# Two x blocks on ScalarE's DMA queue, and the last block's gate quarters in one piece

## The chip, the cores and the metric

The kernel runs on one core of a Trainium2 chip. The metric is the device time of one execution in microseconds (us); the median of three runs before the change is 233.98 us (233.82 to 234.45).

The core has five engines that run side by side, each through its own list of instructions in order: TensorE (PE in the profile, with PEld for its weight loads), VectorE (DVE), ScalarE (ACT), GpSimd (POOL) and SyncE (SP), which here only issues DMAs. ScalarE can issue DMAs as well; its queue is ACTq in the profile, SyncE's is SPq. Both queues are worked off by the same 16 DMA engines.

## The reference

Two branches are computed from x (2048 rows, 640 columns) and added to it. xn is the layer norm of x over its columns.

```python
xn = _layernorm(x, axis=-1)
return x + _A_ref(xn, A_k, A_v, A_shift_k, A_ssm_k, A_ssm_D) + _B_ref(xn, B_w_gate, B_w_up, B_w_down)
...
g = jnp.einsum("bsd,df->bsf", x, w_gate)
u = jnp.einsum("bsd,df->bsf", x, w_up)
h = _sigmoid(g) * u
return jnp.einsum("bsf,fd->bsd", h, w_down)
```

Branch B (the einsums, in which x stands for xn) is a gated layer of width 1728. Branch A shifts k by 0 to 3 rows with four taps a column, multiplies by v, convolves the result along the rows with a kernel as long as the sequence (in the reference by FFT), adds a term with D, and multiplies by xn.

## The kernel before

The 2048 rows are held as 16 blocks of 128 rows, and the blocks in four groups of four. For each group the kernel makes xn, turns it so that columns lie on the partitions (xnT, which has room for one group and four blocks in it), multiplies by the gate and up weights in 14 column groups of 128 (`product`, L267: five matmuls over 640 columns = five chunks of 128), takes the sigmoid of the gate product on ScalarE (`gate_ev`, L278), multiplies it by the up product on VectorE (`up_ev`, L285), and multiplies the result by the down weights (`down_mm`, L309). Branch A runs between these: a long convolution made of matmuls by tables, with transposes through DRAM, in five chunks of 128 columns.

From L543 on the order of all work is written out by hand: `chains` holds lists of steps, and a long string of letters (ORDER) takes the next step of one list after another. The change touches nothing of it. What it touches lies ahead of that, in the start (L501 to L540):

- x's blocks 0 and 1 are loaded in two halves each, one half from SyncE and one from ScalarE (L501 to L503). Block 2 is loaded whole by SyncE and block 3 whole by ScalarE (L504, L505). Behind them SyncE issues the first weights: gate and up for columns 0 to 255, then gate and up for 256 to 511 (L506 to L508; the DMAs are at L177 and L180 in `load_w`). All later loads are SyncE's too.
- `busy(10)` (L522) runs ten matmuls on zeros while the first data is on its way.
- L523 to L529: for blocks 0 to 3, VectorE takes the statistics of the block (`ln_stats`, L200, two instructions), normalises the block before it (`ln_xn`, L217), and combines the statistics (`ln_aggr`, L204); GpSimd makes the reciprocal root (`ln_pow`, L212).
- `turn(i)` (L517) transposes block i on PE in five matmuls against the identity (`xn_mm`, L242, tile pt) and copies them to xnT on ScalarE in two pieces, chunks 0 to 2 and chunks 3 and 4 (`xn_ev`, L246).
- L532 to L537: `quarters(u, i, lo, hi)` (L255, matmuls at L262) computes a quarter of four products, namely block i's 128 rows for the first two column groups (fc 0 and 1), with gate weights for u = 0 and up weights for u = 1, over chunks lo to hi - 1. For each block the gate products of chunks 0 to 2 come first, then the transposes of the next block, then the gate products of chunks 3 and 4, then the up products. Each fc has its PSUM tile, pg for gate and pu for up.
- Then `gate_ev` and `up_ev` for the two column groups (L538 to L540), and the ordered part begins with the gate product of the third column group.

The products' PSUM tiles come from a pool with four buffers (`psG`, L92). After the start, all four are taken: two pg and two pu. The third column group's gate product (L271) takes the first one that comes free, which is pg of fc 0, when its sigmoid has read it.

For the second to fourth group, xnT is not made on PE but by DMA transposes that SyncE issues (`xn_turn`, L250), each behind its block's xn.

Of the kernel before, what the change touches and what calls it, by code (L numbers as in the profile page):

```python
# [21 lines left out]
NC = DM // P  # L22
# [35 lines left out]
def kernel(  # L58
# [14 lines left out]
    nc = tc.nc  # L73
    xr = A_q.flatten_outer_dims().rearrange("(p b) d -> p b d", b=NB)
# [30 lines left out]
    x = res.tile([P, NB, DM], BF16, name="x")  # L105
# [19 lines left out]
    sync = nc.sync  # L125
# [113 lines left out]
    def xn_mm(i):  # L239
        xts[i] = pt = psC.tile([P, NC, P], BF16, name="pt", tag="c")  # L240
        for c in range(NC):
            nc.tensor.transpose(pt[:, c, :], xn[:, i, c * P:(c + 1) * P], ident[:])  # L242

    def xn_ev(i):
        for lo, hi in ((0, 3), (3, NC)):
            nc.scalar.copy(out=xnT[:, i, lo:hi, :], in_=xts[i][:, lo:hi, :])  # L246
# [8 lines left out]
    def quarters(u, i, lo, hi):  # L255

        for fc in range(2):
            if i == 0 and lo == 0:
                pgs[u, fc] = psG.tile([P, 512], F32, name=("pg", "pu")[u], tag="g")
            o = u * UP + fc * P  # L260
            for c in range(lo, hi):
                nc.tensor.matmul(pgs[u, fc][:, i * P:(i + 1) * P], lhsT=w[:, c, o:o + P], rhs=xnT[:, i, c, :],  # L262
                                 start=(c == 0), stop=(c == NC - 1))
# [237 lines left out]
    for b in range(2):  # L501
        for i in range(2):
            (sync, nc.scalar)[i].dma_start(x[:, b, 320 * i:320 * i + 320], xr[:, b, 320 * i:320 * i + 320])  # L503
    for i in range(2):  # L504
        (sync, nc.scalar)[i].dma_start(x[:, 2 + i, :], xr[:, 2 + i, :])  # L505
    for lo in (0, 256):  # L506
        for u in range(2):
            load_w(sync, lo, lo + 256, u)  # L508
# [8 lines left out]
    def turn(i):  # L517
        xn_mm(i)
        xn_ev(i)
# [10 lines left out]
    turn(0)  # L530
    busy(2)
    for i in range(4):  # L532
        quarters(0, i, 0, 3)
        if i < 3:
            turn(i + 1)
        quarters(0, i, 3, NC)
        quarters(1, i, 0, NC)  # L537
    for fc in range(2):  # L538
        gate_ev(0, fc)
# [162 lines left out]
```

## Time and profile before

| what | value |
|---|---|
| median of three runs | 233.98 us |
| the profiled execution's own time | 234.07 us |
| its span, first to last instruction | 232.3 us |
| PE busy | 227.5 us (98% of the span), 2200 matmuls |
| DVE busy | 203.4 us (88%) |
| ACT busy | 123.2 us (53%) |
| granted TensorE clock | 1.00 |
| DMA | 56.79 MB, mean 244 GB/s |
| first x half issued, first bytes | 0.72 us, from 1.75 us |
| first gate weights issued, landed after | 2.12 us, 4.7 us |
| first up weights issued, first up product | 2.60 us, 8.02 us |
| first 512-wide product | 12.67 us |

How to read the profile: times are counted from the start of the span. "L262" is line 262 of the kernel as printed above. A tile name such as pg<-xnT,w tells what an instruction writes and reads. The chain of waits is followed back from the last instruction to whatever released it, so that it shows the one path that set the end. A timeline lists instructions in order of time, with start, duration, engine, line and tiles; like instructions are merged (x5), and in square brackets is the idle time before, with what ended it. A matmul's end is modelled, and matmuls overlap in the pipeline: a 128-wide one is shown as 0.22 us, while in a run of them the next begins 0.056 us after the last. So a short wait of PE can lie hidden under the shown end of the matmul before. DMA share is the busy share of the 16 DMA engines; it can be over 1, since packets overlap.

### The profile page before, as it was taken

The page shows a single profiled execution, that of the slowest core. Times are in us where ns is not written, and L with a number is a line of the kernel's source. Part 1 is how long each engine was busy: PE and PEld are TensorE (multiplying, and loading weights), DVE is VectorE, ACT ScalarE, POOL GpSimd, SP SyncE. Part 2 cuts the span into 40 slices and gives each one's busy share as a digit, 9 for nine tenths or more (in the row PEclk, how much of TensorE's full clock was granted, in tenths as well). Part 3 has the DMA queues.
Part 4 walks back from the last instruction along what each step waited for, and adds up shares of the span by engine and source line. Part 5 has one row for each costly group of instructions (what it writes and reads, how often), then busy time and mean ns, then how long its engine had stood idle before and what let it go on. Part 6 is the DMA issues. An engine that isn't in the chain of part 4 may idle for free.

```text
span 232.3 us, 5434 instructions
## 1 busy us (share of the span) xinstructions
PE 227.5 (98%) x2200; PEld 130.7 (56%) x2200; DVE 203.4 (88%) x357; ACT 123.2 (53%) x158; POOL 12.4 (5%) x26
## 2 busy tenths in 40 slices
PE   7899999999999999999999999999999999999995
PEld 2754445877454556667554544478653544446772
DVE  4534799999989999999999999997799999997773
ACT  2533232595355887766775847673556667752000
POOL 5210010040001100000011000000000000000000
PEclk9999999999999999999999999999999999999999
DMA  6999999899999999999999999689999999364784
GB/s 177 321 328 234 265 305 298 210 226 175 337 192 296 265 324 224 265 210 233 302 293 266 262 259 286 193 204 178 302 257 264 274 270 257 114 167 118 228 261 136
DMA packets 96303, 56.79 MB, mean 244 GB/s; under 512 B 55894, under 2 KB 90518, under 8 KB 96022
## 3 DMA queue, kind: packets, MB, share of 16 engines
q1 hardware_dynamic: 95846, 56.12, 93.9%
q8 instruction: 17, 0.28, 0.5%
q10 hardware_dynamic: 432, 0.33, 0.5%
q14 instruction: 8, 0.07, 0.1%
HBM read 36.12 MB, written 18.35 MB: 234 GB/s over the span
## 4 chain that ended last, share of the span: by engine, by line
PE 95%; DMA 2%; SPq 1%; issue 0%; DVE 0%
PE pd L315 27%; PE pg L271 24%; PE pu L271 24%; PE psb L488 4%; PE ps L376 4%; PE ps L374 4%; PE ps L418 3%; PE psa L447 2%; DMA w<-in_B_w_up_dram 2%; PE pg L292 2%; PE pu L262 1%; PE pg L262 1%; SPq L503 0%; PE pt L242 0%; SPq L177 0%; SPq L505 0%
## 5 line engine op out<-in xcount | busy, mean ns | idle before, releaser
L271 PEld LDWEIGHTS <-w 128*128 128x128 bf16 x500 | 46.6, 98 | 54.3 <-issue 4.6
L315 PE MATMUL pd<-wd,hT 128*128 128x320 bf16 (+2 forms) x448 | 66.0, 299 | 0.0
L271 PE MATMUL pg<-xnT,w 128*128 128x512 bf16 x250 | 62.2, 379 | 0.1
L271 PE MATMUL pu<-xnT,w 128*128 128x512 bf16 x250 | 62.2, 379 | 0.0
L315 PEld LDWEIGHTS <-hT 128*128 128x128 bf16 x448 | 41.7, 98 | 18.2 <-issue 2.4
L280 ACT ACTIVATE sig<-pg 128x512 bf16<-128x512 f32 x52 | 31.1, 601 | 30.8 <-PE pg L271 25.5
L286 DVE TENSOR_TENSOR hT<-sig,pu 128x512 bf16<-128x512 bf16 x52 | 34.9, 680 | 11.8 <-PE pu L271 7.3
L232 ACT CAST xz<-ps 128x1024 bf16<-128x1024 f32 x36 | 35.1, 1015 | 15.5 <-PE ps L418 15.4
L232 ACT CAST t<-ps 128x1024 bf16<-128x1024 f32 x24 | 23.7, 1013 | 16.3 <-PE ps L376 14.1
L433 DVE TENSOR_TENSOR xz<-xz 128x2048 bf16<-128x2048 bf16 x20 | 24.4, 1219 | 0.2
L376 PE MATMUL ps<-kvh,S1t 128*128 128x128 bf16 x160 | 21.5, 220 | 0.0
L374 PE MATMUL ps<-kvh,S1t 128*128 128x128 bf16 x160 | 21.4, 218 | 0.0
L354 DVE TENSOR_TENSOR acc<-acc,tmp 128x1024 bf16<-128x1024 bf16 x30 | 20.5, 683 | 0.3
L352 DVE TENSOR_TENSOR tmp<-kx,sc 128x1024 bf16<-128x1024 bf16 x30 | 20.4, 680 | 0.3
L320 DVE TENSOR_TENSOR x<-pd,x 128x320 bf16<-128x320 f32 (+2 forms) x32 | 15.2, 482 | 3.8 <-PE pd L315 3.6
L374 PEld LDWEIGHTS <-S1t 128*128 128x128 bf16 x160 | 15.5, 97 | 2.5
L376 PEld LDWEIGHTS <-S1t 128*128 128x128 bf16 x160 | 15.4, 96 | 2.5
L232 ACT CAST TBt<-ps 128x1024 bf16<-128x1024 f32 x14 | 13.8, 1012 | 4.0 <-PE ps L376 4.0
L200 DVE BATCH_NORM_STATS2 st<-x 128x6 f32<-128x320 bf16 x32 | 13.8, 474 | 2.2 <-DMA x<-in_A_q_dram 2.1
L493 DVE TENSOR_TENSOR yx<-psb,xn 128x512 bf16<-128x512 f32 x20 | 13.7, 687 | 1.4 <-PE psb L488 0.8
L431 DVE STREAM_SHUFFLE xz<-xz 128x512 f32<-128x512 f32 x20 | 14.5, 726 | 0.0
L232 ACT CAST ao<-psa 128x1024 bf16<-128x1024 f32 x9 | 9.0, 1013 | 8.6 <-PE psa L447 6.9
(56 smaller groups left out, 159.0 us busy)
## 6 DMA issues: line engine op xcount, KB each, us to landing
t<-d SPq DMA_DIRECT2D x15, 512.0 KB, 6.4
d<-t SPq DMA_DIRECT2D x13, 512.0 KB, 5.0
d<-TBt SPq DMA_DIRECT2D x7, 512.0 KB, 5.2
d<-ao SPq DMA_DIRECT2D x6, 512.0 KB, 6.5
bi<-d SPq DMA_DIRECT2D x6, 512.0 KB, 5.5
kx<-in_A_k_dram SPq DMA_DIRECT2D x10, 256.0 KB, 6.0
hn<-in_A_ssm_k_dram SPq DMA_DIRECT2D x20, 128.0 KB, 5.3
kvh<-in_A_v_dram SPq DMA_DIRECT2D x10, 256.0 KB, 5.6
```

The lines of the kernel that those rows point to most:

```text
L232: nc.scalar.copy(out=out, in_=in_)
L271: nc.tensor.matmul(pg[:, :], lhsT=w[:, c, u * UP + fc * P:u * UP + (fc + 1) * P], rhs=xnT[:, :, c, :], start=(c == 0), stop=(c == NC - 1))
L280: nc.scalar.activation(sig[fc][:, :], pgs[0, fc][:, :], ACT.Sigmoid)
L286: nc.vector.tensor_tensor(hT[:, fc, :], sig[fc][:, :], pgs[1, fc][:, :], ALU.mult)
L315: nc.tensor.matmul(pd[:, :], lhsT=hT[:, fc, bb * P:(bb + 1) * P], rhs=wd[:, fc, es], start=(fc == 0), stop=(fc == NFC - 1))
L320: nc.vector.tensor_tensor(x[:, 4 * t + bb, es], pds[bb, half][:, :], x[:, 4 * t + bb, es], ALU.add)
L352: nc.vector.tensor_tensor(d["tmp"][:, :, :], kx[:, lo + 3 - m:hi + 3 - m, :], sb(m), ALU.mult)
L354: nc.vector.tensor_tensor(d["acc"][:, :, :], d["acc"][:, :, :], d["tmp"][:, :, :], ALU.add)
L374: nc.tensor.matmul(ps[:, i, 0:P], lhsT=S1[:, b, h, :], rhs=cin[c]["kvh"][:, 0, b, :], start=True, stop=True)
L376: nc.tensor.matmul(ps[:, i, P:2 * P], lhsT=S1[:, b, h, :], rhs=hp[:, b // 2, b % 2, :], start=True, stop=True)
L431: nc.vector.stream_shuffle(z[:, 2, :, :].bitcast(F32), z[:, 1, :, :].bitcast(F32), swap)
L433: nc.vector.tensor_tensor(z[:, 1:3, :, :], z[:, 0:1, :, :].to_broadcast((P, 2, 8, P)), z[:, 1:3, :, :], ALU.mult)
```

## The change

x's third and fourth blocks (2 and 3) are both loaded by ScalarE, behind the two halves that it loads already; SyncE goes from its halves of blocks 0 and 1 straight to the first gate weights. And for the last of the four blocks, which has no next block to transpose, the gate quarters are taken over all five chunks at once: all five chunks of fc 0, then all five of fc 1, where before chunks 0 to 2 of both came ahead of chunks 3 and 4 of both.

```diff
     for b in range(2):
         for i in range(2):
             (sync, nc.scalar)[i].dma_start(x[:, b, 320 * i:320 * i + 320], xr[:, b, 320 * i:320 * i + 320])
-    for i in range(2):
-        (sync, nc.scalar)[i].dma_start(x[:, 2 + i, :], xr[:, 2 + i, :])
+    for b in range(2, 4):
+        nc.scalar.dma_start(x[:, b, :], xr[:, b, :])
...
     for i in range(4):
-        quarters(0, i, 0, 3)
         if i < 3:
+            quarters(0, i, 0, 3)
             turn(i + 1)
-        quarters(0, i, 3, NC)
+            quarters(0, i, 3, NC)
+        else:
+            quarters(0, i, 0, NC)
         quarters(1, i, 0, NC)
```

The number of DMAs, their sizes and the number of matmuls stay as they are.

## The prediction

> **What bounds the kernel now.** I read the page's busy shares and slices first, then the chain of waits over the whole span and over its first 14 us, then DMA in stretches of 0.25 us, then the timelines of the engines at the places that the chain named. The page (PE's slices, and the chain's shares):
>
> ```profile
> PE   7899999999999999999999999999999999999995
> ...
> PE 95%; DMA 2%; SPq 1%; issue 0%; DVE 0%
> ```
>
> TensorE (PE) is nearly always busy, and 95% of the chain that ended last is its own work. What can be won lies where the chain is not PE, and that is its first 8 us. The chain of waits for 0 to 14 us (start, duration, what):
>
> ```profile
> 1.66 0.42 SPq L505
> 2.08 0.04 issue
> 2.12 0.43 SPq L177
> 2.56 0.04 issue
> 2.60 5.37 DMA w<-in_B_w_up_dram
> 7.97 0.05 issue
> 8.02 0.73 PE pu L262 x10
> ...
> 12.10 0.56 PE pu L262 x10
> 12.66 0.01 issue
> 12.67 1.24 PE pg L271 x5
> ```
>
> Read upwards: the first up products start at 8.02, when the first up weights have landed; these were issued at 2.60, behind the gate weights (2.12), behind x's third block (L505, 1.66) on SP's queue. From 8.02 on the chain is PE. The waits list gives PE one wait on a weight DMA before that, 0.5 us at the first gate products (6.89).
>
> **Part 1, x's blocks and SP's queue.** SP issues one DMA less before the weights: 2.12 - 1.66 = 0.46 us. Gate weights go out at 1.66, up weights at 2.14, and so do all later SP issues until the queue is full. If landing follows issue, up lands at 7.51: a gain of 0.46. If the DMA engines are full throughout, no byte arrives sooner in sum, and the gain is 0. The DMA stretches decide (stretch, its length, busy us of PE, PEld, DVE, ACT, POOL, granted clock, DMA share, GB/s):
>
> ```profile
> 3.00:3.25 0.25, 0.25 (x2) 0.01 (x1) 0.15 (x1) 0.00 (x0) 0.03 (x1) 1.00 1.10 192
> 3.25:3.50 0.25, 0.25 (x2) 0.15 (x1) 0.25 (x1) 0.00 (x0) 0.00 (x0) 1.00 0.74 97
> 3.50:3.75 0.25, 0.25 (x2) 0.04 (x1) 0.25 (x2) 0.00 (x0) 0.00 (x0) 1.00 0.78 179
> 3.75:4.00 0.25, 0.25 (x2) 0.11 (x1) 0.24 (x1) 0.00 (x0) 0.00 (x0) 1.00 0.73 261
> ...
> 5.00:5.25 0.25, 0.25 (x2) 0.00 (x0) 0.25 (x1) 0.00 (x0) 0.00 (x0) 1.00 1.07 333
> ```
>
> Between 3.25 and 3.75 the engines move 97 and 179 GB/s, against 333 later: (333 - 97 + 333 - 179) x 0.25 = 98 KB are missing, which is 0.29 us at 333 GB/s. In this dip x's third block is alone at the head of SP's queue, with the gate weights behind it; after the change the gate weights are at the head there. First bytes follow an issue by 1.03 us (first issue 0.72, first bytes from 1.75), so that gate data can flow from about 2.7. I take the **0.29 us** of the dip, between the ends of 0 and 0.46, because it is the room that the rows show.
>
> The Trainium skill ("DMA: Bandwidth & Descriptors", section "Issuing engines are not separate DMA queues") speaks against this part: transfers issued from different engines share the same 16 DMA engines, and a second issuer saves its sequencer's time alone. By it the dip is not filled by a change of queue and the term would be 0 instead of 0.29; the rows from 5.00 on (share over 1) agree with it, the dip does not settle it.
>
> What the step brings with it:
> - ScalarE's queue issues x's fourth block at 2.11 instead of 1.65, and ends at 2.57. ScalarE's next real work is the copy at 5.99, before which it sat idle 3.35 us: cost 0.
> - The fourth block landed at 1.65 + 4.3 = 5.95; its statistics start at 7.03, so it may come 1.08 later. It goes out 0.46 later and now shares the engines with gate weights. If it came as late as the gate weights do today (2.12 + 4.7 = 6.82) it would still be in time: cost 0. Later than 7.03 it holds up VectorE, and, since xn's third block is ready at 8.23 and PE's transposes of it would then start at 8.87 - 0.29 = 8.58, holds up PE from about 7.4 on, one for one.
> - The third block (landed 1.66 + 4.1 = 5.76) ended a VectorE wait of 0.17 at 5.75. It can come a little sooner or later; PE has 0.2 to 0.4 us over at each transpose. Cost 0, with 0.17 either way.
> - What is late next, once the weights come 0.29 sooner: the gate products would start at 6.60, behind the copies of block 0 (the first is done by 6.5). The transposes of block 1 wait for xn (6.55 + 0.43 = 6.98), so they start near 7.05; four more gate products end near 7.55; the up products take their place at 7.73. So the 0.29 goes through; weights ahead by more than about 0.45 would find PE waiting for xn instead.
> - Second weights (256 to 511) land at 3.75 + 6.4 = 10.15, and are needed at 12.67: no effect.
>
> **Part 2, the last block's gate quarters whole.** The 40 gate matmuls stay, 0.056 us apart; the order changes for block 3. Before, chunks 0 to 2 of both column groups come first, then 3 and 4, so that group 0 ends with the eighth matmul; now it ends with the fifth, 3 x 0.056 = 0.17 sooner. That matters, because group 0's sigmoid holds the PSUM buffer of the next product (four buffers, all taken). ScalarE's timeline (start, duration, what):
>
> ```profile
> 11.17 0.38 ACT L246 COPY xnT<-pt 128x256 bf16<-128x256 bf16 x1
> ...
> 12.03 0.60 ACT L280 ACTIVATE sig<-pg 128x512 bf16<-128x512 f32 x1 [0.48 <-PE pg L262]
> ```
>
> The sigmoid ends at 12.63 and the product starts at 12.67, where PE could have gone on at 11.94 + 10 x 0.056 = 12.50: a stall of 0.17 that the list of waits hides, since the last matmul's modelled end lies over it. What is added: chunk 3 of group 0 is reached at 11.38 + 3 x 0.056 = 11.55, and its copy ends at 11.17 + 0.38 = 11.55, so it waits about 0.04 (the step from sigmoid to product). Behind it in PE's queue stand all later products, so they pay it. Net **0.13 us** gained. Bounds: 0.17 if the copy is in time; a loss of 0.1 if it comes 0.2 to 0.3 late (no row shows that).
>
> **What comes after.** A gain at the start counts only if nothing later holds PE. By the spacing of its matmuls PE has one further wait. The timeline of PE (start, duration, what):
>
> ```profile
> 56.28 1.11 PE L315 MATMUL pd<-wd,hT 128*128 128x320 bf16 x7
> 57.44 1.24 PE L271 MATMUL pg<-xnT,w 128*128 128x512 bf16 x5
> ```
>
> Seven matmuls 0.136 apart from 56.28 let the next start at 57.23; it starts at 57.44, 0.21 late. It needs the second row group's xnT, whose last DMA transpose SP issues at 54.7, with 2.8 us to landing for the quickest: about 57.4. So this landing must move too. SP's four transposes start at 49.49, behind xn of VectorE (48.98 + 0.44 = 49.42). VectorE has no gap from 30.21 to there, and its instruction at 30.21 waited for PE's up product (end 30.10). So the landing hangs on PE and moves with it, 0 lost; bounds are the whole gain lost, and 0.21 more gained where it moves by more.
>
> **Sum.** 234.07 (the profiled execution; its span is 232.3, with 1.8 around it) - 0.29 - 0.13 = 233.65. The median of the three runs is 233.98, so that this execution lies 0.09 above it; I give **233.6**. A difference under 0.3% (0.70 us) is about what a measurement of this kernel cannot tell from no change.
>
> **Rivals.**
> - Bytes bind, the queue doesn't (the change doesn't do what it says): SP issues sooner, the weights land when they did. For it: DMA share over 1 from 5.00 to 8.00, and all of x, the gate and the up weights stand before PE's 8.02 in either order. Against: the dip. 234.07 - 0.13 = 233.94. This is also the time by the skill's sentence above.
> - The gain is swallowed at 57.44: xnT's last block lands when it did, for DMA reasons. For: SP's first transpose took 2.47 us to issue where the others took 1.22, so the queue is full there. Against: VectorE's gapless run. 234.07.
> - Slower, by the same place: one more of the four transposes takes the 2.47 us of the first, and the last lands 1.25 later, at 58.65. It decides as soon as the last landing comes after PE's own 57.23 less the gain; then every 0.1 costs 0.1. 234.07 + 1.25 = 235.3.
> - More: up lands by the full 0.46 sooner, the copy is in time (0.17), and xnT beats PE (0.21): 234.07 - 0.84 = 233.2.
>
> **Chances.** Forecast 0.40 (gains of 0.2 to 0.7), bytes bind 0.15, swallowed 0.14, more 0.16, slower 0.15. The first three lie within 0.3%, except 0.02 of the forecast that is faster and 0.01 of the swallowed case that is slower: faster 0.18, same 0.66, slower 0.16. The range goes from the case "more", less 0.2 for what the third x block could add, to 0.6 above the swallowed case, half-way into the slower one: 232.9 to 234.6.
>
> **What the changed profile would show.** Step 1: L177's first issue at 1.66, the wait at the first up products ending near 7.7, no dip at 3.25 to 3.75; x's fourth block's statistics still at about 7.0. Step 2: the first sigmoid 0.13 ahead of its place relative to the last quarter, and no gap at the first 512-wide product. Afterwards: the product at 57.44 near 57.0. Wrong it would be if up's landing stays near 7.97, if VectorE waits for the fourth block, or if the product at 57.44 does not move with the start.

## The result, and the profile after

The changed kernel takes 235.25 us (median of 6 runs, 235.01 to 235.87); the kernel before takes 233.96 us (233.82 to 234.45, 6 runs). The ratio is 1.0058, with a 95% interval of 1.0042 to 1.0074: slower by about 1.3 us. The forecast was 233.6 us, and the range ended at 234.6. The profiled execution of the changed kernel took 235.72 us, with a span of 233.9 us (before 234.07 and 232.3).

The page of the changed kernel, PE's slices and the chain's shares:

```profile
PE   7699999999999999999999999999999999999995
...
PE 94%; DMA 4%; DVE 1%; issue 0%
```

PE is as full as before from the third slice on. What is new stands in the first slices: the chain has 4% of DMA in it, where before it had 2%. The chain of waits of the changed kernel for 0 to 14 us (start, duration, what):

```profile
0.72 2.64 DMA x<-in_A_q_dram
3.35 0.02 issue
3.38 5.94 DMA x<-in_A_q_dram
9.32 0.02 issue
9.34 0.89 DVE st L200 x2
10.23 0.36 DVE xn L217
10.59 0.05 issue
10.63 0.45 PE pt L242 x5
...
11.31 0.56 PE pu L262 x10
```

The up weights are gone from the chain. In their place stand two loads of x, one behind the other: the first half block, issued at 0.72, lands at 3.36; only then, at 3.38, is another load of x issued, and it takes 5.94 us, to 9.32. The timeline of the changed kernel names the second one (start, duration, engine, line, tiles, idle time before):

```profile
1.65 0.46 ACTq L505 DMA_DIRECT2D x<-in_A_q_dram  x1
2.69 0.65 SPq L177 DMA_DIRECT2D w<-in_B_w_gate_dram  x1
3.38 0.40 ACTq L505 DMA_DIRECT2D x<-in_A_q_dram  x1
6.96 0.51 PE L262 MATMUL pg<-xnT,w 128*128 128x128 bf16 x6 [0.53 <-DMA w<-in_B_w_gate_dram]
9.34 0.89 DVE L200 BATCH_NORM_STATS2 st<-x 128x6 f32<-128x320 bf16 x2 [1.74 <-DMA x<-in_A_q_dram]
10.14 0.43 DVE L217 TENSOR_SCALAR xn<-x,mv,rstd 128x640 bf16<-128x640 bf16 x1
10.63 0.45 PE L242 MATMUL pt<-ident,xn 128*128 128x128 bf16 x5 [1.48 <-DVE xn L217]
```

ScalarE issues x's third block (block 2) at 1.65 and ends at 2.11; the fourth (block 3) does not follow there but at 3.38. In between, at 2.69, the second gate weights have gone out on SyncE's queue. (L177 and L180 in `load_w` are the same lines for the first and the second weights; the issue at 1.66, not shown, is the first gate weights'.) VectorE stands 1.74 us at the statistics of block 3. Behind them in its queue is the xn of block 2 (10.14), whose data had long been there, and PE waits 1.48 us for that xn. The first 512-wide product starts at 14.28 instead of 12.67, 1.61 late, and this is still there at the second row group. The timeline of PE in the changed kernel:

```profile
57.89 1.11 PE L315 MATMUL pd<-wd,hT 128*128 128x320 bf16 x7
59.09 1.24 PE L271 MATMUL pg<-xnT,w 128*128 128x512 bf16 x5
```

59.09 less 57.44 is 1.65, and the span is 1.6 longer. So the whole loss is made in the first 11 us, and it is still there at the end.

**Why 3.38.** The compiled order of instructions (place on the engine, line, what it waits for) says it. Before, on SyncE:

```text
3 L177 DMACopy w_82<-in_B_w_gate_dram 128x5x256
4 L180 DMACopy w_82<-in_B_w_up_dram 128x5x256
5 L177 DMACopy w_82<-in_B_w_gate_dram 128x5x256 [waits DMAHW0_49]
6 L180 DMACopy w_82<-in_B_w_up_dram 128x5x256 [waits DMAHW1_49]
```

After, on SyncE and on ScalarE:

```text
4 L177 DMACopy w_82<-in_B_w_gate_dram 128x5x256
5 L180 DMACopy w_82<-in_B_w_up_dram 128x5x256 [waits DMAHW1_49]
...
4 L503 DMACopy x_79<-in_A_q_dram 128x320
5 L505 DMACopy x_79<-in_A_q_dram 128x640
6 L505 DMACopy x_79<-in_A_q_dram 128x640 [waits DMAHW0_49]
```

The compiled program signals the landing of these DMAs by eight semaphores, DMAHW0 to DMAHW7, handed out in turn to the DMAs of both queues. The ninth DMA gets DMAHW0 again and waits until its first user has landed. Before, the ninth was the second gate weights (issued at 3.34, needed at 12.67: no harm). After, it is x's block 3, since in the order in which the semaphores are handed out it now stands behind the second gate weights. So the change moved a wait that was there already to another load, and by it let the second gate weights go out ahead of that load.

### The profile page after: what moved, and what is told of

It is laid out like the page before. It is cut to its first block, busy times and chain, and to the rows that moved or that the text cites. A ratio compares the mean times of both kernels' runs of the same rounds, so it can differ in the third digit from the quotient of the medians.

```text
span 233.9 us, 5434 instructions
## 1 busy us (share of the span) xinstructions
PE 227.7 (97%) x2200; PEld 130.7 (56%) x2200; DVE 203.2 (87%) x357; ACT 123.2 (53%) x158; POOL 12.4 (5%) x26
## 4 chain that ended last, share of the span: by engine, by line
PE 94%; DMA 4%; DVE 1%; issue 0%
PE pd L315 26%; PE pu L271 23%; PE pg L271 23%; PE psb L488 4%; PE ps L376 4%; PE ps L374 4%; DMA x<-in_A_q_dram 4%; PE ps L418 3%; PE psa L447 2%; PE pg L292 2%; PE pu L262 1%; PE pg L262 1%; DVE st L200 0%; PE pt L242 0%; DVE xn L217 0%; DVE x L320 0%
```

## The experiments

The texts on record name the theories by letters. At first: the wait for the semaphore makes block 3 late (W); it is late by the company that it keeps, behind block 2 on one queue and beside the weights on the same DMA engines, whenever it is issued (S); the quarters of part 2 cost the time (Q). Later came: a transfer is served in order of issue, by the bytes ahead of it (F), or by the pieces ahead of it (N); and the landings near 43 us are a floor under any earlier start (D). Ratios are to the kernel before, measured beside it on the same chip, with 95% intervals.

**e1: part 1 alone.** The quarters stay as before.

```diff
-    for i in range(2):
-        (sync, nc.scalar)[i].dma_start(x[:, 2 + i, :], xr[:, 2 + i, :])
+    for b in range(2, 4):
+        nc.scalar.dma_start(x[:, b, :], xr[:, b, :])
```

> Part 1 alone (x's blocks 2 and 3 on ScalarE's queue; gate quarters as before). The trace of the changed kernel shows x's block 3 issued at 3.38 us, not 2.11, and its statistics at 9.34, not 7.03. Theory W (wait): that issue waits for the landing of ScalarE's first x half, since it takes over that DMA's completion semaphore. Rival S (sharing): block 3 would come late on that queue at any issue time, because it shares the DMA engines with the weights. Rival Q (quarters): the slowdown is due to the new order of the last gate quarters. W and S: about 0.12 us slower than the changed kernel, 235.4 us. Q: no slower than before, 234.0 us or less.

Measured: 235.04 us against 234.23, ratio 1.0039 (1.0026 to 1.0052). Block 3 was issued at 3.19 and landed at 8.67; PE waited 1.37 us for xn. The loss belongs to part 1, and the quarters are cleared of it: the intervals of e1 and of the whole change overlap.

**e2: part 2 alone.**

```diff
     for i in range(4):
-        quarters(0, i, 0, 3)
         if i < 3:
+            quarters(0, i, 0, 3)
             turn(i + 1)
-        quarters(0, i, 3, NC)
+            quarters(0, i, 3, NC)
+        else:
+            quarters(0, i, 0, NC)
```

> Part 2 alone (the last block's gate quarters whole; x's blocks as before). W and S: about 0.12 us faster than before, 233.85 us (the first 512-wide product 1.18 us after the last gate quarter's start instead of 1.29). Q: slower by about 1.3 us, 235.2 us.

Measured: 234.12 us against 234.23, ratio 0.9994 (0.9976 to 1.0013). In its profile the first 512-wide product starts at 12.26, 0.41 ahead of the kernel before: 0.11 by the shorter way from the last gate quarter to the product (1.18 against 1.29), 0.30 because the quarter itself began sooner in this execution. Yet the second group's product starts at 57.54, not ahead of 57.44. The timelines of VectorE and PE in this run show where the 0.41 went:

```profile
42.20 1.11 DVE L334 STREAM_TRANSPOSE kvh<-hn 128x512 f32<-128x512 f32 x1 [0.30 <-DMA hn<-in_A_ssm_k_dram]
43.77 0.89 DVE L200 BATCH_NORM_STATS2 st<-x 128x6 f32<-128x320 bf16 x2 [0.45 <-DMA x<-in_A_q_dram]
...
54.72 0.23 PE L374 MATMUL ps<-kvh,S1t 128*128 128x128 bf16 x1 [0.55 <-DVE kvh L357]
```

VectorE waits twice for loads, the second time for x's second group (L133, issued at 35.73 here, at 36.17 before: sooner by 0.44; landed 8.01 later, while before VectorE took it up 7.21 after its issue without a wait). PE then waits 0.55 for VectorE. The expected gain of about 0.12 us in the total is less than the interval can show.

**e3: block 3 with a semaphore of its own.** Changed kernel; ScalarE's warm-up sigmoid (L123) stands behind its DMAs instead of between them, which changes the order in which the semaphores are handed out.

```diff
-    nc.scalar.activation(warm[:, :], mhalf[:, :], ACT.Sigmoid)
...
     for b in range(2, 4):
         nc.scalar.dma_start(x[:, b, :], xr[:, b, :])
+    nc.scalar.activation(warm[:, :], mhalf[:, :], ACT.Sigmoid)
```

> The changed kernel, with the warm-up sigmoid of ScalarE moved behind its four x DMAs. By the compiled order of instructions x's block 3 then has a completion semaphore that no earlier DMA used, and the wait goes to the third weight DMA, as before the change; queues, sizes and order of the x DMAs stay. W: block 3 is issued near 2.1 us, lands by 7.1, the PE stall at its transposes' predecessors is gone; 233.8 us (before less 0.12 of part 2, nothing from the weights, which landed no sooner in the changed kernel). S: block 3 still lands after 8.5 us, 234.8 us or more.

Measured: 234.06 us, ratio 0.9998 (0.9981 to 1.0015). The timeline:

```profile
1.65 1.01 ACTq L504 DMA_DIRECT2D x<-in_A_q_dram  x2
3.16 0.37 SPq L176 DMA_DIRECT2D w<-in_B_w_gate_dram  x1
7.33 0.89 DVE L199 BATCH_NORM_STATS2 st<-x 128x6 f32<-128x320 bf16 x2 [0.43 <-DMA x<-in_A_q_dram]
```

Blocks 2 and 3 go out one behind the other from 1.65 on, the second gate weights wait again (3.16), and VectorE waits 0.43 instead of 1.74. The loss is gone: S, with the same bytes in the same queues, falls. What is left is no gain either. The first product started at 12.46, and then VectorE waited 0.61 for x's second group at 43.76 and PE 0.34 for kvh at 54.71, as in e2.

**e4: the wait put into the kernel before.** A 192-byte load on ScalarE's queue ahead of block 3 makes block 3 the ninth DMA; queues and quarters are those of before. The bytes go to a place that the kernel fills later anyway.

```diff
-    for i in range(2):
-        (sync, nc.scalar)[i].dma_start(x[:, 2 + i, :], xr[:, 2 + i, :])
+    sync.dma_start(x[:, 2, :], xr[:, 2, :])
+    nc.scalar.dma_start(TBt[0:1, 0, 0:3, 0:32], SMd.ap()[0:1, :, :])
+    nc.scalar.dma_start(x[:, 3, :], xr[:, 3, :])
```

> The kernel before, with one DMA of 192 bytes more on ScalarE's queue ahead of x's block 3 (into a place that is loaded over later). Queues as before: block 2 on SyncE, block 3 on ScalarE, weights behind block 2. By the compiled order of instructions, block 3 now is the DMA that has to wait for ScalarE's first x half. W: issued near 3.4 us, lands at 8.5 to 9.3, PE stalls 0.8 to 1.6; 234.7 to 235.5 us. S: as before, 234.0 us.

Measured: 234.07 us, ratio 0.9999 (0.9983 to 1.0015). The expectation failed. The timeline:

```profile
3.15 0.34 ACTq L506 DMA_DIRECT2D x<-in_A_q_dram  x1
3.29 0.52 SPq L177 DMA_DIRECT2D w<-in_B_w_gate_dram  x1
7.75 0.89 DVE L200 BATCH_NORM_STATS2 st<-x 128x6 f32<-128x320 bf16 x2 [1.06 <-DMA x<-in_A_q_dram]
```

Block 3 does wait, and goes out at 3.15, but it lands 4.6 us later (e1: 5.5, changed kernel: 5.9). So the wait is not the whole cause. Two things differ from the changed kernel: block 2 is on SyncE's queue here, and the second gate weights go out behind block 3 (3.29) and not ahead of it (2.69). e5 leaves block 2 on ScalarE's queue and so tells them apart.

**e5: changed kernel, second weights behind block 3.** The same small load, now on SyncE's queue between the first and the second weights, so that the second gate weights wait too.

```diff
     for lo in (0, 256):
         for u in range(2):
             load_w(sync, lo, lo + 256, u)
+        if lo == 0:
+            sync.dma_start(TBt[0:1, 0, 0:3, 0:32], SMd.ap()[0:1, :, :])
```

> The changed kernel with a DMA of 192 bytes more on SyncE's queue, between the first and the second weights. It takes the last unused completion semaphore, so that the second gate weights, too, wait for a landing and go out at about the same time as x's block 3, not 0.7 us ahead of it. The wait of block 3 itself stays (issue near 3.2 to 3.4 us). Putting the wait into the kernel before cost nothing, so the wait alone is not enough. Theory F (first come, first served): both queues' transfers are served nearly in the order of issue, and block 3 lands behind all bytes issued before it; up's landing (1280 KB at 7.97) and block 3's in the kernel before (640 KB at 5.95) give 324 GB/s. F here: 1280 KB up to and with block 3, landing 7.6 to 8.3, PE held 0 to 0.4; 234.0 to 234.3 us. Rival W (the wait alone, on this queue): lands 8.7 to 9.3 as in the changed kernel; 235.2 us.

Measured: 234.08 us against 234.14, ratio 0.9992 (0.9973 to 1.0011). The timeline:

```profile
2.95 0.33 ACTq L505 DMA_DIRECT2D x<-in_A_q_dram  x1
3.57 0.38 SPq L177 DMA_DIRECT2D w<-in_B_w_gate_dram  x1
7.84 0.89 DVE L200 BATCH_NORM_STATS2 st<-x 128x6 f32<-128x320 bf16 x2 [0.96 <-DMA x<-in_A_q_dram]
```

The wait is there (2.95 instead of 2.11), the second weights are behind, and the loss is gone. Block 3 landed at 7.82, as F expected (7.6 to 8.3) and W did not (8.7 to 9.3). It lands 1.50 sooner than in the changed kernel, of which 0.43 is its earlier issue. e3 takes away the wait and with it the overtaking (the second weights going out ahead of block 3); e5 takes away the overtaking and keeps the wait. Either removes the loss. The overtaking without the wait was not tried, so whether it alone would make the loss stays open.

**e6: more bytes ahead.** Changed kernel with the second weights 512 columns wide (640 KB instead of 320 KB each), so that twice as much goes out between the up weights and block 3.

```diff
-    for lo in (0, 256):
+    for lo, hi in ((0, 256), (256, 768)):
         for u in range(2):
-            load_w(sync, lo, lo + 256, u)
+            load_w(sync, lo, hi, u)
...
-    for k in ((load_w, sync, 512, 1024, 0),
-              (load_w, sync, 512, 1024, 1),
+    for k in ((load_w, sync, 768, 1024, 0),
+              (load_w, sync, 768, 1024, 1),
```

> The changed kernel with second weights twice as wide (columns 256 to 767, then 768 to 1023 behind them): 640 KB instead of 320 KB go out between the up weights and x's block 3. Issue of block 3 as in the changed kernel. F: 328 KB more at 324 GB/s, 1.0 us later than in the changed kernel: lands near 9.7 to 10.3; 236.2 us. W: as the changed kernel, 235.2 us.

Measured: 235.31 us, ratio 1.0042 (1.0027 to 1.0057). The timeline:

```profile
9.02 0.89 DVE L200 BATCH_NORM_STATS2 st<-x 128x6 f32<-128x320 bf16 x2 [2.25 <-DMA x<-in_A_q_dram]
```

Issued at 3.18, landed at 8.99: 5.8 us, no more than with half the bytes ahead (5.5 in e1, 5.9 in the changed kernel). F, which asked for 1.0 us more in the landing and in the total, fails: the ratio lies between those of e1 (1.0039) and of the changed kernel (1.0058).

**e7: part 2, and x's second group in two loads.** This asks whether the landings near 43 us swallow the gain of e2. Against e2 the edit is:

```diff
-              (load_x, sync, 1),
+              (load_x, sync, 1, 2),
```

> Part 2 alone, and x's second group of four blocks loaded as two DMAs of two blocks instead of one of four. In the run of part 2 alone, the first 512-wide product came at 12.25 instead of 12.67 us, but VectorE then waited 0.30 for hn and 0.45 for x's second group (statistics at 43.77; 43.38 in the kernel before), and PE 0.55 near 54.7 for VectorE: the gain of the start was gone. Theory D: these landings, set by the bytes of the DMA queue up to there, are a floor that the start does not move. With the first two blocks landing about 1 us sooner the second wait goes, 0.30 is left of hn: 0.1 to 0.4 us faster than part 2 alone, 233.6 to 233.9 us. Rival: the floor is elsewhere (kv of branch A), and this changes nothing, 234.0 us.

Measured: 233.68 us, ratio 0.9981 (0.9965 to 0.9997), the only version whose interval lies wholly below 1. The timelines of VectorE and PE:

```profile
43.01 0.85 DVE L200 BATCH_NORM_STATS2 st<-x 128x6 f32<-128x320 bf16 x2
...
56.03 1.11 PE L315 MATMUL pd<-wd,hT 128*128 128x320 bf16 x7
56.98 1.24 PE L271 MATMUL pg<-xnT,w 128*128 128x512 bf16 x5
```

The statistics start at 43.01 without a wait, and the product starts 0.95 after the seven down matmuls (7 x 0.136), where before it took 1.16. In this execution it is 0.46 ahead of 57.44, and the span is 231.8 against 232.3. Two parts make up the 0.46. The first product came at 12.42, 0.25 ahead of before, and the seven down matmuls too are 0.25 ahead (56.03 against 56.28): this lead was kept. The other 0.21 is the shorter step behind the down matmuls, which e8 shows without part 2 as well.

**e8: the two loads alone**, on the kernel before: the diff of e7, without part 2.

> The kernel before, with x's second group loaded as two DMAs of two blocks. VectorE had no wait at 43.38 in the kernel before. D: no change, 233.8 to 234.0 us. If x's landing already held the kernel before there, up to 0.2 faster.

Measured: 233.84 us, ratio 0.9986 (0.9972 to 1.0000). By the medians the split alone brings 0.30 of e7's 0.46 us, but the intervals of e7 and e8 overlap. Its profiled execution started late (first product at 13.03), so the trace shows one thing only: the product follows the down matmuls by 0.95 here too (56.64 to 57.59), so that this 0.21 belongs to the two loads and not to part 2.

**e9: as many bytes ahead, in longer pieces.** Changed kernel with 320 KB of x, in 128 pieces of 2560 bytes (blocks 4 and 5), issued between the up weights and the second gate weights, which have pieces of 512 bytes.

```diff
     for lo in (0, 256):
         for u in range(2):
             load_w(sync, lo, lo + 256, u)
+        if lo == 0:
+            sync.dma_start(x[:, 4:6, :], xr[:, 4:6, :])
...
-              (load_x, sync, 1),
+              (sync.dma_start, x[:, 6:8, :], xr[:, 6:8, :]),
```

> The changed kernel with half of x's second group (blocks 4 and 5: 320 KB as 128 pieces of 2560 bytes, which is loaded later otherwise) put between the first and the second weights on SyncE's queue. It goes out ahead of x's block 3, where the changed kernel has the second gate weights (320 KB as 640 pieces of 512 bytes); those now go out with block 3. Doubling their bytes at the same number of pieces moved block 3's landing to 8.99, not to the 9.7 to 10.3 of theory F, so F's bytes are not what counts ahead of block 3. Theory N: the place in line is given by pieces (rows to be written), first come, first served. N: block 3 lands at 7.8 to 8.3, little later than with nothing there (7.82); 234.0 to 234.4 us. F: 8.7 to 9.3, as with 320 KB of weights; 235.1 us.

Measured: 235.06 us against 234.75, ratio 1.0031 (1.0013 to 1.0048). The timeline:

```profile
9.20 0.89 DVE L200 BATCH_NORM_STATS2 st<-x 128x6 f32<-128x320 bf16 x2 [2.12 <-DMA x<-in_A_q_dram]
```

Issued at 3.29, landed at 9.18: 5.9 us. Fewer pieces don't help, and N falls.

**e10: half the bytes ahead in as many pieces.** Changed kernel with the second weights in two steps of 128 columns (160 KB each, 640 pieces of 256 bytes).

```diff
-    for lo in (0, 256):
+    for lo, hi in ((0, 256), (256, 384), (384, 512)):
         for u in range(2):
-            load_w(sync, lo, lo + 256, u)
+            load_w(sync, lo, hi, u)
```

> The changed kernel with the second weights cut into columns 256 to 383 and 384 to 511: ahead of x's block 3 go 160 KB of gate weights as 640 pieces of 256 bytes, instead of 320 KB as 640 pieces of 512. N: block 3 lands as in the changed kernel and in part 1 alone, 8.6 to 9.3; 235.0 us. F: half-way to the kernel with nothing there (7.82), 8.2 to 8.5; 234.6 us.

Measured: 235.51 us against 234.75, ratio 1.0035 (1.0016 to 1.0054). The timeline:

```profile
8.76 0.89 DVE L200 BATCH_NORM_STATS2 st<-x 128x6 f32<-128x320 bf16 x2 [1.73 <-DMA x<-in_A_q_dram]
```

Issued at 3.10, landed at 8.74: 5.6 us. That lies in N's range (8.6 to 9.3) and not in F's (8.2 to 8.5), but e9 had already spoken against N. Its span is 234.1, the longest of all, though its first product (13.70) started before that of the changed kernel: SyncE has two more loads to issue, x's second group came late (VectorE waited 0.78 for it at 45.44), and PE waited 0.77 at 56.39. This part of its time says nothing on block 3.

The runs side by side, in us from the start of the span, from the timelines and chains. The landing is read where VectorE waited for it; before, it is the issue and the 4.3 of the list of DMAs. "Between" is what went out on SyncE's queue after the up weights and before block 3.

| run | block 3 issued | between | landed | issue to landing | first 512-wide product | second group's | span |
|---|---|---|---|---|---|---|---|
| before | 1.65 | (up comes later) | 5.95 | 4.3 | 12.67 | 57.44 | 232.3 |
| e4 | 3.15 | nothing | 7.73 | 4.6 | 12.81 | 57.45 | 232.2 |
| e5 | 2.95 | 192 bytes | 7.82 | 4.9 | 12.78 | 57.34 | 232.1 |
| e3 | about 2.1 | nothing | 7.31 | 5.2 | 12.46 | 57.53 | 232.4 |
| e1 | 3.19 | 320 KB, 640 pieces | 8.67 | 5.5 | 13.75 | 58.31 | 233.2 |
| e10 | 3.10 | 160 KB, 640 pieces | 8.74 | 5.6 | 13.70 | 59.21 | 234.1 |
| e6 | 3.18 | 640 KB, 640 pieces | 8.99 | 5.8 | 13.95 | 58.51 | 233.3 |
| e9 | 3.29 | 320 KB, 128 pieces | 9.18 | 5.9 | 14.14 | 59.15 | 233.9 |
| after | 3.38 | 320 KB, 640 pieces | 9.32 | 5.9 | 14.28 | 59.09 | 233.9 |

All runs with one large transfer between land at 8.67 to 9.32, all without at 7.82 or sooner. Neither the bytes nor the pieces of that transfer order the five; e1 and the changed kernel, whose loads are the same up to there, landed 0.65 apart, so single executions could not show a smaller effect of size. By what rule the DMA engines serve the two queues stays open; what the runs show is that one more large transfer issued ahead on the other queue cost block 3 about 1 us (from issue to landing 5.5 to 5.9, against 4.6 and 4.9 in e4 and e5).

The Trainium skill ("DMA: Bandwidth & Descriptors", section "Queues, rings and completion order") says that each DMA engine goes round its queues packet by packet. By that, block 3 would take turns with SyncE's transfers as soon as block 2, ahead of it on ScalarE's queue, is through. That the price does not grow from 160 to 640 KB agrees with it; that one transfer ahead on the other queue costs about 1 us does not follow from it.

## Why the prediction was wrong

**The step that failed** is "ScalarE's queue issues x's fourth block at 2.11 ... cost 0". Its reasoning went by ScalarE's own time: the issue before ends at 2.11, and ScalarE has nothing else to do. It left out that a DMA also needs its semaphore. Block 3 went out at 3.38, 1.27 later than forecast, and behind the second gate weights, which the step did not count as going ahead of it; it landed at 9.32, where the step allowed 6.82. The trace of before held a sign of it: SyncE issued the first up weights at 2.60, done at 3.13, but the second gate weights only at 3.34, and the list of waits had 0.2 us of L177 on a DMA of x. The timeline of before:

```profile
2.60 0.53 SPq L180 DMA_DIRECT2D w<-in_B_w_up_dram  x1
3.34 0.37 SPq L177 DMA_DIRECT2D w<-in_B_w_gate_dram  x1
```

It had no place in the sum. In e4 and e5 the wait alone, without the weights going ahead, cost nothing that the total shows (ratios 0.9999 and 0.9992). What made the loss is what the wait lets happen: the second gate weights go first, and block 3 then lands about 1 us later than behind the wait alone.

**The price, once late, was right.** The prediction had block 3 hold up PE "from about 7.4 on, one for one" against transposes at 8.58. A landing at 9.32 then gives 8.58 + 1.92 = 10.50; the transposes started at 10.63. On PE's timeline the same transposes started at 8.92 before (8.87 is their weight load), so they were 1.71 late; 0.11 of it came back by part 2, and the first product was 1.61 late. The condition was written down, and a wait of VectorE for the fourth block was named as a sign of being wrong, but no rival was made of it, and no chance was given to a landing as late as this.

**The weights, forecast -0.29.** The reason given for this term failed; its size is not settled. The reason was that the gate weights fill the dip in DMA traffic. DMA in stretches of 0.25 us in the changed kernel (columns as in the prediction):

```profile
3.25:3.50 0.25, 0.25 (x2) 0.15 (x1) 0.25 (x1) 0.00 (x0) 0.00 (x0) 1.00 0.71 85
3.50:3.75 0.25, 0.25 (x2) 0.04 (x1) 0.25 (x2) 0.00 (x0) 0.00 (x0) 1.00 0.47 95
3.75:4.00 0.25, 0.25 (x2) 0.11 (x1) 0.25 (x1) 0.00 (x0) 0.00 (x0) 1.00 0.63 183
```

The dip is still there (85, 95 and 183 GB/s against 97, 179 and 261), and it is no gap in SyncE's queue: weights stood issued from 1.66 on. It is there in e1, e3, e6, e9 and e10 too (76 to 116 GB/s at 3.25 to 3.50), but not in e5 (254). Why it is there stays open. The rule of the Trainium skill ("DMA: Bandwidth & Descriptors", section "Issuing engines are not separate DMA queues") that the prediction named does not let a change of queue fill the dip, and the trace of the changed kernel agrees with that.

Whether the weights came sooner is another question, and the changed kernel's one trace cannot answer it. Its gate products waited for weights until 6.96 (before 6.89). Its first up products, at 8.09 (before 8.02), did not wait for the up weights: they stood behind the transposes of block 1, which waited for xn, since VectorE had waited 0.61 for block 2, until 6.23. Such a late block 2 is not the change's doing alone: in e8, where SyncE loads it as before, VectorE waited for it until 6.24. The traces of all runs can be put side by side. In all of them PE's first load of gate weights waited for the DMA, so that its start is the landing; the first up product is no earlier than the landing of the up weights.

| traces | first gate weights issued | first load of gate weights on PE | first up product |
|---|---|---|---|
| block 2 ahead of the weights (before, e2, e4, e7, e8) | 2.11 to 2.15 | 6.25 to 7.24, median 6.75 | 7.72 to 8.37, median 8.02 |
| part 1 (changed kernel, e1, e3, e5, e6, e9, e10) | 1.63 to 1.67 | 6.13 to 6.95, median 6.37 | 7.25 to 8.09, median 7.67 |

For example, before and in e1:

```profile
6.88 0.34 PEld L262 LDWEIGHTS <-w 128*128 128x128 bf16 x6 [0.99 <-DMA w<-in_B_w_gate_dram]
...
6.37 0.10 PEld L262 LDWEIGHTS <-w 128*128 128x128 bf16 x1 [0.27 <-DMA w<-in_B_w_gate_dram]
7.56 0.72 PE L262 MATMUL pu<-xnT,w 128*128 128x128 bf16 x10
```

With part 1 the medians are 0.38 and 0.35 sooner, close to the forecast 0.29, but the ranges overlap, and these kernels differ in more than this. So neither the 0.29 nor the 0 of the rival "bytes bind" is shown. In e3 and e5, which have part 1 without the loss, no gain is left in the total (ratios 0.9998 and 0.9992).

**The quarters, forecast -0.13.** Right in size. The timeline of the changed kernel:

```profile
13.10 0.77 PE L262 MATMUL pg<-xnT,w 128*128 128x128 bf16 x10
13.63 1.09 ACT L280 ACTIVATE sig<-pg 128x512 bf16<-128x512 f32 x2 [0.36 <-PE pg L262]
...
14.28 1.02 PE L271 MATMUL pg<-xnT,w 128*128 128x512 bf16 x4
```

From the last gate quarter to the first product it takes 1.18, where before it took 1.29 (11.38 to 12.67): 0.11. But in e2 the total does not show it (ratio 0.9994), and its trace shows the lead lost before the second group.

**What comes after, forecast "moves with it, 0 lost".** Right for the loss, which was still there in full; not so for the gains of e2 and e3. The step followed xn back through a VectorE without gaps and concluded that the landing hangs on PE. But a queue without gaps does not tell how much sooner its loads would be there. VectorE's timeline of before:

```profile
42.26 1.10 DVE L334 STREAM_TRANSPOSE kvh<-hn 128x512 f32<-128x512 f32 x1
43.38 0.89 DVE L200 BATCH_NORM_STATS2 st<-x 128x6 f32<-128x320 bf16 x2
```

The instruction at 43.38 started right behind the one before it (42.26 + 1.10 = 43.36). In e2 and e3, which came there sooner, it had to wait for x's second group until 43.77 and 43.76. How long before 43.38 that load had landed in the kernel before, no trace shows; in e2 and e3 it landed later than that. A first product earlier by 0.2 to 0.4 thus ended 0.1 behind 57.44. With that load in two pieces (e7) a lead of 0.25 was kept, and 0.21 came on top. So a gain of 0.13 and 0.29 would probably not have come through in full, and for an earlier start the rival "swallowed" had the right result with another place: x's second group at 43, not the transposes' DMAs at 57. That 43 is where it is swallowed rests on two profiled executions with the wait and on e7, whose ratio lies only just below 1, beside e8, which has most of that gain without part 2.

**Slower** had a chance of 0.15 as a rival, by a late transpose at 57.44. The changed kernel is slower, but not by that mechanism: the product at 59.09 follows the down matmuls by 1.20, about as before (1.16). That the prediction had some chance for a slower kernel is luck in this respect.

## What to carry to other kernels

Before moving a DMA to another queue, count it among all DMAs in flight: where completion semaphores are handed out in turn, the wait of the ninth falls on another transfer when the order changes, and the compiled order of instructions names it without a run. Then ask not only when the moved transfer could go out, but what goes out ahead of it while it waits. A stretch of an engine without idle time is no proof that it could have started sooner: look at the landing of each load that it reads, since an earlier start can run into one. And do not read a shift of some tenths of a us in a landing from one pair of traces: in e1 and the changed kernel, with the same loads, block 3 landed 0.65 apart.

## What the runs showed that was not expected

- One large transfer issued ahead on the other queue made 160 KB land 8.67 to 9.32 us after the start instead of 7.73 or 7.82, and 160, 320 or 640 KB, in 128 or 640 pieces, made no ordered difference.
- The dip in DMA traffic at 3.25 to 3.75 us was there with a different transfer at the head of SyncE's queue, and was gone in e5, where a load of 192 bytes stood between the first and the second weights.
- A load of x issued 0.44 us sooner (35.73 against 36.17, e2) was taken up 0.39 us later (43.77 against 43.38).
